# A retention layer's states kept as two 64x64 blocks per pair of heads, with half-array and quarter-array matmuls

## The chip, the cores and the metric

The kernel runs on one core of a Trainium2 chip. The time is device microseconds of that core for one launch; several runs are taken and their median is given. The profile is one execution of the program, recorded by the hardware profiler. Its engines are called PE (TensorE, the matrix engine; PEld are its weight loads), DVE (VectorE), ACT (ScalarE), POOL (GpSimd) and SP (SyncE, which issues transfers).

## The reference

The first half is a linear recurrence over time with a decay per head. Its result, all heads side by side, goes through a two-layer network without bias.

```python
batch, n_heads, seq, head_dim = (4, 8, 768, 64)      # q, k, v, fp32
gamma = 1.0 - 2.0 ** (-5.0 - np.arange(H))
for t in range(S):
    state = gamma * state + einsum('bhd,bhe->bhde', k[:, :, t], v[:, :, t])
    y[:, :, t] = scale * einsum('bhd,bhde->bhe', q[:, :, t], state)
x = y.transpose(0, 2, 1, 3).reshape(B * S, H * D)    # 3072 x 512
h = x @ w_in                                         # 512 x 2048
g = h * tanh(softplus(h))
out = g @ w_out                                      # 2048 x 512, fp32
```

A state belongs to one batch and one head and has 64 x 64 numbers.

## The kernel before

The recurrence is computed in chunks of 128 time steps: 6 chunks per batch, 24 in all, numbered g. The 8 heads are handled as 4 pairs (HP = 4), two heads of 64 side by side on the 128 partitions. Products use 16-bit floats and are summed in fp32 in PSUM. For each chunk:

- `casts` (L211) brings q, k, v to fp16 with the decay multiplied in; POOL does most of it. `turn_k`, `turn` or `turn_by_dma` (L202, L255, L227) transpose q and k.
- `scores` (L266) multiplies k and q of each head: 8 matmuls that use 64 rows of the array, two at a time on different rows. `mask` (L277, DVE) keeps the causal part.
- `outer` (L288) forms k times v over the chunk. Before, one matmul per pair of heads makes a 128x128 block on the whole array. Its diagonal 64x64 blocks are the products of the two heads; the other two blocks mix heads and aren't wanted.
- `state` (L299, DVE) adds the state before (`su`, L306) and multiplies by `gcm` (L307, or L303 alone for the first chunk of a batch and in the first block). `gcm` holds the decay of 128 steps in the diagonal blocks and zero elsewhere, so that it also clears the unwanted blocks. In the first block the state before is added on PE instead, by a matmul with the identity (L296).
- `past` (L310) multiplies the state before with q: one whole-array matmul per pair of heads, 128 columns moving.
- `present` (L317) multiplies the masked scores with v: one matmul per head with a stationary operand of 64 columns, on the left or right half of the array, two side by side.
- ACT copies the sum of past and present from PSUM to `xt` (L349, L358, L400), the input of the network.

The network runs in blocks: the first has 4 chunks, each of the other 10 has 2. `g1` (L405) is the first layer with Mish on ACT (L420). The second layer is `g2_mm` (L424) in blocks 0 to 2. Blocks from 3 on (`SEVEN`) use `seven` (L486), which multiplies 2x2 blocks with seven products and sums `gsum` on DVE (L475 to L484). The sums of the weights are made once (L459 to L462).

The order on each engine is that of the program text; nothing reorders it. The work on chunks stands between the dense matmuls of the block before. Blocks 1 and 2 follow `plan_of` (L646): `scores_two` and `outer_two` among the dense products, then `y_two` (past and present). From block 3 on, `outer_two` comes after the first step of g1, `scores_two` after the fourth, and `y_two` inside `seven`. In the first block (`first_block`, L570) the four chunks go one by one while the weights are still on their way; identity matmuls without use (`spin`, and `spin_quarters`, L247, which works on quarters of the array) keep PE busy there. `last_of_batch` skips the outer product of a batch's last chunk, so that some groups have one chunk and some two. PSUM tiles come from two pools, `mmps` with 4 banks and `atps` with 2 tiles of two banks each, the latter for scores, outer products and y of later chunks.

Of the kernel before, what the change touches and what calls it, by code (L numbers as in the profile page):

```python
# [9 lines left out]
FP16 = mybir.dt.float16  # L10
FP32 = mybir.dt.float32
# [5 lines left out]
def kernel(  # L17
# [9 lines left out]
    nc = tc.nc  # L27
    B, H, S, D = q.shape
    d_model, d_ff = moe_w_in.shape
    P = 128  # L30
    C = 128
    NCH = S // C
    NCK = B * NCH
    HP = H // 2
# [12 lines left out]
    gamma = (1.0 - 2.0 ** (-5.0 - np.arange(H))).astype(np.float64)  # L47
# [7 lines left out]
    cpool = ctx.enter_context(tc.tile_pool(name="rn_const", bufs=1))  # L55
# [4 lines left out]
    stp = ctx.enter_context(tc.tile_pool(name="rn_state", bufs=3))  # L60
# [4 lines left out]
    mmps = ctx.enter_context(  # L65
        tc.tile_pool(name="rn_mmps", bufs=4, space=bass.MemoryType.PSUM))
    atps = ctx.enter_context(
        tc.tile_pool(name="rn_atps", bufs=2, space=bass.MemoryType.PSUM))
# [6 lines left out]
    qs_spread = qvs[:, 2 * H:].rearrange("p (r h) -> p h r", r=CPB)  # L75
    ident = cpool.tile([P, P], FP16, name="ident")
    tri = cpool.tile([P, C], FP32, name="tri")
    gcm = cpool.tile([P, HP, P], FP32, name="gcm")
    warm = cpool.tile([P, 1], FP32, name="warm")
    nc.gpsimd.memset(ident, 0.0)  # L80
    nc.gpsimd.affine_select(  # L81
# [11 lines left out]
        pattern=[[-1, CPB], [-CPB, C // CPB]], channel_multiplier=1)  # L93
    nc.vector.memset(warm, 0.0)
    nc.scalar.activation(warm, warm, AF.Mish)
    nc.vector.memset(gcm, 0.0)
    for h in range(H):
        o = 64 * (h % 2)
        nc.vector.memset(gcm[o:o + 64, h // 2, o:o + 64], float(gamma[h] ** C))

    win_ap = moe_w_in.rearrange("(bp p) f -> p bp f", p=P)
    wout_ap = moe_w_out.rearrange("(fb p) c -> p fb c", p=P)
# [2 lines left out]
    loaded, cast, qkts, ats, ams, states, us, ys = {}, {}, {}, {}, {}, {}, {}, {}  # L105
# [182 lines left out]
    def outer(g, u_ps, onto=None):  # L288
        _, k16, v16, _ = cast[g]
        for i in range(HP):  # L290
            nc.tensor.matmul(  # L291
                u_ps[:, i], k16[:, 2 * i:2 * i + 2], v16[:, 2 * i:2 * i + 2],
                start=onto is None or i == 0, stop=onto is None,
                skip_group_check=onto is not None)
        if onto is not None:
            nc.tensor.matmul(u_ps, ident, onto, start=False, stop=True, skip_group_check=True)  # L296
        us[g] = u_ps

    def state(g):  # L299
        u_ps = us.pop(g)  # L300
        st = stp.tile([P, HP, P], FP16, name="st")
        if g % NCH == 0 or g < CPB:
            nc.vector.tensor_tensor(st, u_ps, gcm, op=ALU.mult)  # L303
        else:
            su = stp.tile([P, HP, P], FP32, name="su")
            nc.vector.tensor_tensor(su, u_ps, states[g - 1], op=ALU.add)  # L306
            nc.vector.tensor_tensor(st, su, gcm, op=ALU.mult)  # L307
        states[g] = st

    def past(g, y, fresh, pairs=range(HP)):  # L310
        st, qt = states[g - 1], qkts[g][0]
        for i in pairs:
            nc.tensor.matmul(  # L313
                y(i), st[:, i], qt[:, i], start=fresh(i), stop=False,
                skip_group_check=True)

    def present(g, y, fresh, pairs=range(HP)):  # L317
        am = ams[g]
# [8 lines left out]
    def last_of_batch(g):  # L327
        return g % NCH == NCH - 1
# [2 lines left out]

    def outer_one(g):
        if not last_of_batch(g):
            outer(g, mmps.tile([P, HP, P], FP32, name="u_ps", tag="mm"), states.get(g - 1))

    def xt_first(g, pairs=slice(None)):
        n = C // CPB
# [3 lines left out]
    def y_one(g):  # L341
        y_ps = mmps.tile([P, HP, C], FP32, name="y_ps", tag="mm")
        inter = g % NCH > 0
        if inter:
            past(g, lambda i: y_ps[:, i], lambda i: i == 0)
        present(g, lambda i: y_ps[:, i], lambda i: not inter and i == 0)
        if g == 0:
            xts[0] = xtp.tile([P, HP, TB], FP16, name="xt")
        nc.scalar.copy(xt_first(g), y_ps.rearrange("p i (r c) -> p i r c", r=CPB))  # L349

    def y_one_in_halves(g):
        n = HP // 2
        y_ps = [mmps.tile([P, n, C], FP32, name="y_ps", tag="mm") for _ in range(2)]
        for k in range(2):
            past(g, lambda i: y_ps[k][:, i % n], lambda i: i % n == 0, range(k * n, (k + 1) * n))
        for k in range(2):
            present(g, lambda i: y_ps[k][:, i % n], lambda i: False, range(k * n, (k + 1) * n))
            nc.scalar.copy(  # L358
                xt_first(g, slice(k * n, (k + 1) * n)),
                y_ps[k].rearrange("p i (r c) -> p i r c", r=CPB))  # L360
# [3 lines left out]
        mask(g)  # L364

    def outer_state(g):
        outer(g, atps.tile([P, 2, HP, P], FP32, name="u_ps", tag="at")[:, 0])
        state(g)


# [8 lines left out]
    def outer_two(blk):  # L379
        a = first[blk]  # L380
        u_ps = atps.tile([P, 2, HP, P], FP32, name="u_ps", tag="at")
        for j in range(2):
            if not last_of_batch(a + j):
                outer(a + j, u_ps[:, j])
        for j in range(2):
            if not last_of_batch(a + j):
                state(a + j)

    def y_two(blk):
        a = first[blk]  # L390
        y_ps = atps.tile([P, HP, 2, C], FP32, name="y_ps", tag="at")
        inter = a % NCH > 0
        if inter:
            past(a, lambda i: y_ps[:, i, 0], lambda i: i % 2 == 0)
        past(a + 1, lambda i: y_ps[:, i, 1], lambda i: not inter and i % 2 == 0)
        for j in range(2):
            present(a + j, lambda i: y_ps[:, i, j], lambda i: False)
        xt = xtp.tile([P, HP, TB], FP16, name="xt")
        xts[blk] = xt
        nc.scalar.copy(  # L400
            xt[:, :, :2 * C], y_ps.rearrange("p i j c -> p i (j c)"))
# [168 lines left out]
    def first_block():  # L570
# [18 lines left out]
        for g in range(CPB):  # L589
            last = g == CPB - 1  # L590
            if not last:
                cast_to(g + 2)
            scores(g)
            mask(g, 2 if last else 1)
            if g > 0:
                y_one(g - 1)
            if not last:
                at_tile(g + 1)
                outer_one(g)
                spin(g + 1, 2 if g else 8)  # L600
                turn_k(g + 1)
                state(g)
                spin_quarters(g + 1, (48, 40, 16)[g], C // 2 if g < 2 else C)
        y_one_in_halves(CPB - 1)
        outer_one(CPB - 1)
        cast_win(0)
        state(CPB - 1)
        for s in range(1, NSL):
# [6 lines left out]
            24: [(turn, CPB)],  # L615
            25: [(scores_one, CPB)],
            27: [(outer_state, CPB)],
            28: [(turn, CPB + 1), (next_chunk, CPB + 2), (next_chunk, CPB + 3)],
            29: [(scores_one, CPB + 1)],
# [26 lines left out]
    def plan_of(blk):  # L646
        a = first[blk] + 4
        if blk >= SEVEN:
            plan = {1: [(cast_to, a + 1), (next_chunk, a)],
                    7: [(cast_to, a + 2), (next_chunk, a + 1)]}  # L650
            if blk + 1 < len(BLOCKS):
                plan[0] = [(outer_two, blk + 1)]
                plan[3] = [(scores_two, blk + 1)]
            return plan
        early, then_seven = blk == 1, blk + 1 == SEVEN
        plan = {1: [(cast_to, a + 1)],
                (1 if early else 2 if then_seven else 4): [(cast_to, a + 1), (next_chunk, a)],
                (5 if early else 8): [(cast_to, a + 2), (next_chunk, a + 1)]}
        plan[10 if early else 7] = [(scores_two, blk + 1)]
        plan[12 if early else 10] = [(outer_two, blk + 1)]  # L660
        plan[14 if early else 13] = [(y_two, blk + 1)]
        return plan
# [58 lines left out]
```

## Time and profile before

| what | value |
|---|---|
| median of 3 runs | 208.84 us (208.76, 208.84, 210.17) |
| span of the profiled execution | 206.5 us; no separate time of that execution is given, and the median is 2.3 us above its span |
| granted PE clock, mean | 0.999 |
| PE busy | 200.1 us in 2005 matmuls |
| first layer, L412 | 88.0 us in 704 matmuls |
| outer products, L291 | 80 matmuls, 219 ns each from issue to end |
| past, L313 | 80 matmuls, 219 ns each |
| present, L323 | 192 matmuls, 219 ns each |
| scores, L273 | 192 matmuls, 216 ns each |
| state, L303, L306, L307 | 7, 13 and 13 operations, 684, 691 and 754 ns each |

Matmuls overlap in the pipeline: a whole-array matmul of 128 columns lasts 219 ns, but the next can start 56 ns later. So what a matmul costs is read from the distance of the starts, and not from its length. Rows such as "128*64 128x128" give the part of the array (rows*columns of the stationary operand) and then the moving operand (partitions x columns).

### The profile page before, as it was taken

The page shows a single profiled execution, that of the slowest core. Times are in us where ns is not written, and L with a number is a line of the kernel's source. Part 1 is how long each engine was busy: PE and PEld are TensorE (multiplying, and loading weights), DVE is VectorE, ACT ScalarE, POOL GpSimd, SP SyncE. Part 2 cuts the span into 40 slices and gives each one's busy share as a digit, 9 for nine tenths or more (in the row PEclk, how much of TensorE's full clock was granted, in tenths as well). Part 3 has the DMA queues.
Part 4 walks back from the last instruction along what each step waited for, and adds up shares of the span by engine and source line. Part 5 has one row for each costly group of instructions (what it writes and reads, how often), then busy time and mean ns, then how long its engine had stood idle before and what let it go on. Part 6 is the DMA issues. An engine that isn't in the chain of part 4 may idle for free.

```text
span 206.5 us, 4747 instructions
## 1 busy us (share of the span) xinstructions
PE 200.1 (97%) x2005; PEld 151.0 (73%) x2005; DVE 120.7 (58%) x184; ACT 86.5 (42%) x146; POOL 76.2 (37%) x72
## 2 busy tenths in 40 slices
PE   7899999999999999999999999999999999999993
PEld 2465444455855865788888888888888888898882
DVE  2697454267019998475585774495675773572062
ACT  2243664142631541453453453453453453552640
POOL 3242000427866555578665265156266000000000
PEclk9999999999999999999999999999999999999999
DMA  5999999999899999999999798499894800200202
GB/s 175 237 219 345 381 387 355 233 296 208 176 205 292 195 228 207 213 238 253 209 218 152 168 195 149 115 246 154 200 241 71 206 0 2 105 0 27 77 25 76
DMA packets 99988, 38.59 MB, mean 187 GB/s; under 512 B 90496, under 2 KB 94080, under 8 KB 99968
## 3 DMA queue, kind: packets, MB, share of 16 engines
q1 hardware_dynamic: 96704, 37.50, 82.4%
q10 hardware_dynamic: 3264, 0.81, 2.4%
q8 instruction: 15, 0.25, 0.5%
q14 instruction: 5, 0.04, 0.1%
HBM read 27.29 MB, written 6.29 MB: 163 GB/s over the span
## 4 chain that ended last, share of the span: by engine, by line
PE 83%; SPq 7%; DMA 5%; DVE 1%; ACT 1%; issue 1%; ACTq 0%
PE h_ps L412 38%; PE o_ps L506 23%; PE o_ps L426 13%; SPq L122 5%; DMA wi<-in_moe_w_in_dram 5%; PE y_ps L323 3%; PE at L273 3%; PE y_ps L313 2%; SPq L140 2%; PE u_ps L291 2%; ACT xt L400 1%; DVE gsum L476 1%; SPq L181 0%; DVE win L157 0%; PE t_ps L261 0%
## 5 line engine op out<-in xcount | busy, mean ns | idle before, releaser
L412 PE MATMUL h_ps<-xt,win 128*128 128x256 f16 (+1 forms) x704 | 88.0, 282 | 0.4 <-ACT xt L400 0.2
L420 ACT ACTIVATE g<-h_ps 128x512 f16<-128x512 f32 x96 | 57.3, 597 | 57.6 <-PE h_ps L412 57.6
L412 PEld LDWEIGHTS <-win 128*128 128x128 f16 x704 | 67.9, 98 | 16.9 <-DVE win L157 0.9
L217 POOL TENSOR_TENSOR qk<-qf,qvs 128x512 f16<-128x512 f32 x20 | 21.5, 1077 | 61.6 <-DMA qf<-in_q_dram 52.3
L283 DVE TENSOR_TENSOR am<-at,tri 128x1024 f16<-128x1024 f32 x20 | 23.7, 1220 | 17.1 <-PE at L273 16.9
L223 POOL TENSOR_TENSOR v<-vf,qvs 128x512 f16<-128x512 f32 x24 | 25.4, 1059 | 18.6 <-DMA vf<-in_v_dram 17.0
L426 PE MATMUL o_ps<-wout,g 128*128 128x512 f16 x128 | 30.1, 380 | 0.0
L222 POOL TENSOR_SCALAR qk<-kf 128x512 f16<-128x512 f32 x18 | 27.7, 1540 | 2.0 <-DMA kf<-in_k_dram 0.7
L506 PEld LDWEIGHTS <-gsum 128*128 128x128 f16 x256 | 24.4, 98 | 3.8 <-DVE gsum L476 0.4
L506 PE MATMUL o_ps<-tmat,gsum 128*128 128x256 f16 x192 | 23.7, 273 | 0.1
L426 PEld LDWEIGHTS <-g 128*128 128x128 f16 x128 | 11.7, 98 | 13.0 <-issue 0.3
L520 DVE TENSOR_TENSOR osb<-o_ps,snap 128x256 f32<-128x256 f32 x24 | 10.1, 422 | 18.8 <-ACT snap L512 15.7
L506 PEld LDWEIGHTS <-g 128*128 128x128 f16 x192 | 18.8, 98 | 2.2
L400 ACT CAST xt<-y_ps 128x1024 f16<-128x1024 f32 x10 | 10.1, 1012 | 21.7 <-PE y_ps L323 21.7
L475 DVE TENSOR_TENSOR gsum<-g 128x512 f16<-128x512 f16 x16 | 7.6, 472 | 13.6 <-ACT g L420 13.6
L506 PE MATMUL o_ps<-wout,g 128*128 128x256 f16 x128 | 15.3, 273 | 0.0
L512 ACT COPY snap<-o_ps 128x256 f32<-128x256 f32 x24 | 8.9, 372 | 14.0 <-PE o_ps L506 14.0
L306 DVE TENSOR_TENSOR su<-u_ps,st 128x512 f32<-128x512 f32 x13 | 9.0, 691 | 4.7 <-PE u_ps L291 4.5
L307 DVE TENSOR_TENSOR st<-su,gcm 128x512 f16<-128x512 f32 x13 | 9.8, 754 | 0.4
L243 PE MATMUL at<-ident 128*128 128x512 f16 (+1 forms) x26 | 8.0, 440 | 1.3 <-POOL ident L81 1.3
L220 ACT ACTIVATE qk<-kf 128x512 f16<-128x512 f32 x6 | 3.8, 630 | 12.4 <-DMA kf<-in_k_dram 12.4
L157 DVE CAST win<-wi 128x1024 f16<-128x1024 f32 x8 | 5.4, 692 | 5.3 <-DMA wi<-in_moe_w_in_dram 5.3
(61 smaller groups left out, 150.0 us busy)
## 6 DMA issues: line engine op xcount, KB each, us to landing
kf<-in_k_dram SPq DMA_DIRECT2D x23, 256.0 KB, 4.9
vf<-in_v_dram SPq DMA_DIRECT2D x23, 256.0 KB, 5.0
out_dram<-osb SPq DMA_DIRECT2D x22, 256.0 KB, 4.0
qf<-in_q_dram SPq DMA_DIRECT2D x19, 256.0 KB, 4.4
wt<-in_moe_w_out_dram SPq DMA_DIRECT2D x3, 1024.0 KB, 10.1
wi<-in_moe_w_in_dram SPq DMA_DIRECT2D x4, 512.0 KB, 6.9
wi<-in_moe_w_in_dram SPq DMA_DIRECT2D x2, 1024.0 KB, 10.3
qfirst<-in_q_dram SPq DMA_DIRECT2D x2, 512.0 KB, 5.0
```

Source lines behind the costliest of these rows:

```text
L122: queue.dma_start(loaded[g][n], (q, k, v)[n][b, :, c * C:(c + 1) * C].rearrange("h p d -> p h d"))
L217: nc.gpsimd.tensor_tensor(q16, qf, qs.unsqueeze(2).broadcast_to((P, H, D)), op=ALU.mult)
L222: nc.gpsimd.tensor_scalar(k16, kf, BOOST, None, op0=ALU.mult)
L223: nc.gpsimd.tensor_tensor(v16, vf, vs.unsqueeze(2).broadcast_to((P, H, D)), op=ALU.mult)
L283: nc.vector.tensor_tensor(am[:, :, i:i + n], at[:, :, i:i + n], keep.unsqueeze(1).unsqueeze(1).broadcast_to((P, 2, n, C)), op=ALU.mult)
L307: nc.vector.tensor_tensor(st, su, gcm, op=ALU.mult)
L400: nc.scalar.copy(xt[:, :, :2 * C], y_ps.rearrange("p i j c -> p i (j c)"))
L412: nc.tensor.matmul(h_ps[:, j], wins[s][f // 2][:, bp, f % 2 * P:(f % 2 + 1) * P], xts[blk][:, bp, :nt], start=(bp == 0), stop=(bp == NBP - 1))
L420: nc.scalar.activation(gt, h_ps, AF.Mish, scale=inv_boost3)
L426: nc.tensor.matmul(o_ps, gts[blk, fb][:, t * P:(t + 1) * P], wouts[s][:, f, cols], start=(fb == 0), stop=(fb == NFB - 1))
L506: nc.tensor.matmul(o_ps, x(f), w(f), start=first and f == 0, stop=f == n - 1, skip_group_check=True)
L520: nc.vector.tensor_tensor(dst, o_ps, plus, op=ALU.add)
```

## The change

A state is kept as 64 columns on 128 partitions: the upper 64 partitions hold one head of the pair, the lower 64 the other. The two unwanted blocks are no longer computed or stored.

- `outer`: two matmuls per pair of heads instead of one, each with 64 stationary columns (one half of the array) and 64 moving columns instead of 128. PE issues 160 of these instead of 80.
- `past`: two matmuls per pair of heads instead of one, each on 64 rows and 64 columns of the array (a quarter), the moving operand still 128 columns. 160 instead of 80.
- `state`, and the identity matmul of the first block: 256 columns instead of 512.
- `gcm` has 256 columns and needs no memset to zero ahead.

The order on the other engines and all transfers stay as they were.

```diff
-    gcm = cpool.tile([P, HP, P], FP32, name="gcm")
+    gcm = cpool.tile([P, HP, D], FP32, name="gcm")
...
-    nc.vector.memset(gcm, 0.0)
     for h in range(H):
         o = 64 * (h % 2)
-        nc.vector.memset(gcm[o:o + 64, h // 2, o:o + 64], float(gamma[h] ** C))
+        nc.vector.memset(gcm[o:o + 64, h // 2], float(gamma[h] ** C))
...
     def outer(g, u_ps, onto=None):
         _, k16, v16, _ = cast[g]
         for i in range(HP):
-            nc.tensor.matmul(
-                u_ps[:, i], k16[:, 2 * i:2 * i + 2], v16[:, 2 * i:2 * i + 2],
-                start=onto is None or i == 0, stop=onto is None,
-                skip_group_check=onto is not None)
+            for hh in range(2):
+                nc.tensor.matmul(
+                    u_ps[64 * hh:64 * hh + 64, i], k16[:, 2 * i + hh], v16[:, 2 * i + hh],
+                    start=i == 0, stop=onto is None, skip_group_check=True)
...
-        st = stp.tile([P, HP, P], FP16, name="st")
+        st = stp.tile([P, HP, D], FP16, name="st")
...
-            su = stp.tile([P, HP, P], FP32, name="su")
+            su = stp.tile([P, HP, D], FP32, name="su")
...
     def past(g, y, fresh, pairs=range(HP)):
         st, qt = states[g - 1], qkts[g][0]
         for i in pairs:
-            nc.tensor.matmul(
-                y(i), st[:, i], qt[:, i], start=fresh(i), stop=False,
-                skip_group_check=True)
+            for hh in range(2):
+                o = slice(64 * hh, 64 * hh + 64)
+                nc.tensor.matmul(
+                    y(i)[o], st[o, i], qt[o, i], start=fresh(i), stop=False,
+                    skip_group_check=True)
...
-            outer(g, mmps.tile([P, HP, P], FP32, name="u_ps", tag="mm"), states.get(g - 1))
+            outer(g, mmps.tile([P, HP, D], FP32, name="u_ps", tag="mm"), states.get(g - 1))
...
-        outer(g, atps.tile([P, 2, HP, P], FP32, name="u_ps", tag="at")[:, 0])
+        outer(g, atps.tile([P, 2, HP, P], FP32, name="u_ps", tag="at")[:, 0, :, :D])
...
-                outer(a + j, u_ps[:, j])
+                outer(a + j, u_ps[:, j, :, :D])
```

## The prediction, made before the result was known

> **What bounds the kernel now.** I read the page first: busy shares, the slices, the chain that ended last.
>
> ```profile
> span 206.5 us, 4747 instructions
> PE 200.1 (97%) x2005; PEld 151.0 (73%) x2005; DVE 120.7 (58%) x184; ACT 86.5 (42%) x146; POOL 76.2 (37%) x72
> PEclk9999999999999999999999999999999999999999
> PE 83%; SPq 7%; DMA 5%; DVE 1%; ACT 1%; issue 1%; ACTq 0%
> ```
>
> The matrix engine (PE) carries 83% of the chain at full granted clock; VectorE, which does the state sums, carries 1%. So the change is worth what it does to PE's own stream, and where. The chain in order of time gives the place:
>
> ```profile
> 16.44 9.41 DMA wi<-in_moe_w_in_dram
> 25.88 0.70 DVE win L157
> 26.63 7.08 PE h_ps L412 x32
> ```
>
> Up to 26.6 us the chain runs through the weight loads; PE waits for the cast of win there. From 26.63 on it is PE almost without a break. What PE does between the dense products is seen in its timeline (start, length, line, operation, array rows*columns, moving shape, count):
>
> ```profile
> 60.85 0.62 PE L273 MATMUL at<-qkt 64*128 64x128 f16 x16
> 61.40 1.90 PE L426 MATMUL o_ps<-wout,g 128*128 128x512 f16 x8
> 63.14 0.61 PE L291 MATMUL u_ps<-v,qk 128*128 128x128 f16 x8
> 63.59 1.89 PE L426 MATMUL o_ps<-wout,g 128*128 128x512 f16 x8
> 65.31 0.39 PE L313 MATMUL y_ps<-qkt,st 128*128 128x128 f16 x4
> 65.63 0.64 PE L323 MATMUL y_ps<-am,v 128*64 128x128 f16 x16
> 66.20 1.04 PE L426 MATMUL o_ps<-wout,g 128*128 128x512 f16 x4
> ```
>
> Lengths overlap, so I use start to start. Eight outer products, full array, neighbours full array: 63.14 to 63.59, 0.45 us, 0.056 each. Four past products: 65.31 to 65.63, 0.32 where 4 x 0.056 = 0.22; the missing 0.10 comes where the array goes from 128*128 to 128*64. Sixteen present products on half arrays: 65.63 to 66.20, 0.57, where eight pairs side by side at 0.056 make 0.45; the missing 0.12 is a slow first pair and the way back to 128*128. So one excursion from full array to half array and back costs about 0.22 us beyond its stream. Eight past and sixteen present products elsewhere say the same:
>
> ```profile
> 94.04 0.61 PE L313 MATMUL y_ps<-qkt,st 128*128 128x128 f16 x8
> 94.58 0.64 PE L323 MATMUL y_ps<-am,v 128*64 128x128 f16 x16
> 95.15 1.05 PE L506 MATMUL o_ps<-tmat,gsum 128*128 128x256 f16 x8
> ```
>
> 94.04 to 95.15 is 1.11 us; the stream is 16 x 0.056 = 0.90; the rest is 0.21. (The first product after it is 0.01 late too, in the starts of the trace, which makes 0.22.) A quarter-array stream of 64 columns stands in the first block:
>
> ```profile
> 11.38 0.58 PE L251 MATMUL at<-ident 64*64 64x64 f16 x48
> 11.97 0.40 PE L273 MATMUL at<-qfirst_t,kt 64*128 64x128 f16 x8
> ```
>
> 48 quarters, four side by side: the last ends at 11.96 and one takes 0.193, so starts spread over 0.39: 12 fours at 0.032 us.
>
> **The change part by part.** *Outer products.* After 26.63 there are ten groups in the chain: four of 4 matmuls (44.5, 84.6, 130.4, 176.0 us) and six of 8 (63.3, 77.8, 99.7, 115.1, 145.5, 160.6), 64 in all, each between full-array products. The stream becomes 64 pairs of 64 columns. No row has this pair. Its bounds: 0.028, half the 0.056 of the 128-column pair, and 0.056, if something other than the columns sets it (the 64-column weight loads of L323 last 109 ns, the 128-column ones of L291 98). I take 0.032, from the quarter matmuls of L251, which load 64 columns of weights and stream 64 columns, as here. Each group gains an excursion, 0.22. A group of 4: 4 x 0.032 + 0.22 = 0.35 against 0.22, +0.13. A group of 8: 8 x 0.032 + 0.22 = 0.48 against 0.45, +0.03. Sum 4 x 0.13 + 6 x 0.03 = +0.70 us. With pairs at 0.028 it is 64 x 0.004 = 0.26 less; at 0.056 64 x 0.024 = 1.54 more.
>
> *Past products.* Ten groups after 26.63 (blocks 1 to 10), 68 full matmuls, become 136 quarter matmuls in pairs, upper left and lower right quarter, still 128 moving columns. Pairs of L273 and L323 with 128 columns keep 0.056, so the stream is unchanged. The order full, half, full becomes full, quarter, half, full: one change of array shape more per group. Every change between shapes in these rows costs about 0.10 with a slow first pair of 0.02: 10 x 0.117 = +1.17 us. From 64*64 to 128*64 the trace has no row; nearest is 64*128 to 128*64 at 12.15 to 12.29 us (11.97 and 4 x 0.056 give 12.20, then 0.09 of nothing). Bounds: 0, if a change between two column-split shapes is free, and 0.117; I take the upper, which is nearest. The Trainium skill, TensorEngine Tiling, Key Properties, says that a change of tiling mode, not merely of the tile, empties the array; by it the term stays 1.17, without it 0.
>
> *First block (before 26.6).* Its three y groups go scores (64*128), past, present: the number of changes stays. Outer products of chunks 1 to 3 follow present products, now in the same shape: a change less going in, one more coming out. The group of chunk 0 gains a change, while PE waits about 0.36 us for v. The identity matmul of L296 loses half of 512 columns three times. I set all this to 0: PE's wait before 26.63 (0.22 us in the starts of the trace) and the DMA behind it hide either sign. Without that cover it would be about +0.1.
>
> *VectorE.* 33 state operations go from 512 to 256 columns. The nearest rows are copies out of PSUM: L432 with 512 columns 686 ns, L518 with 256 columns 425. 33 x 0.26 = 8.6 us of VectorE go, and the 0.49 us memset of gcm. In the waits of before no PE instruction waits for L303, L306 or L307; worth 0 on the chain. One VectorE wait lies on it: gsum L476 before 109.23 us, 1.15 us long instead of some 0.45 while GpSimd ran beside it, about 0.32 us of idle PE.
>
> ```profile
> 107.68 1.22 POOL L223 TENSOR_TENSOR v<-vf,qvs 128x512 f16<-128x512 f32 x1
> 108.03 1.15 DVE L476 TENSOR_TENSOR gsum<-gsum,g 128x512 f16<-128x512 f16 x1
> 109.23 0.33 PEld L506 LDWEIGHTS <-gsum 128*128 128x128 f16 x4 [0.42 <-DVE gsum L476]
> ```
>
> It may vanish or come in another block, as the engines shift: 0, between -0.32 and +0.32.
>
> *Waits and queues.* The instruction lists of the two kernels are the same on ScalarE, GpSimd and SyncE, and no wait is added; nothing is moved past another DMA. What queues behind the emptied array is the next dense product, and behind that ScalarE's Mish, which is idle 58% of the time.
>
> **Sum.** 0.70 + 1.17 = +1.87 us. The profiled span of 206.5 becomes 208.4. The median, 208.84, is 2.3 us more than that span, which I take as the work around it; no separate time of the profiled execution is given, and the runs lie from 208.76 to 210.17. 208.84 + 1.87 = 210.7 us, 0.9% slower.
>
> **Rivals.** (a) *Half pairs set by their weight loads*, 0.056 a pair: +1.54, 212.3 us. For it: loads of 64 columns last longer than those of 128. Against it: L251 gets four such loads through in 0.032.
>
> (b) *Quarters that don't run side by side.* In the past products both row halves now write the same bank, in different partitions. In L273 the two row halves write different banks, in L251 too, so no row excludes that the pair is serialised: 68 x 0.056 = +3.8 more, 214.5 us. For it: only the absence of a row. Against it: L323's column halves share a bank at 0.056 a pair. The Trainium skill, TensorEngine Tiling, Restrictions and Gotchas, says that different row tiles can't access one PSUM bank at the same time; taken literally it gives this rival's time. No run here shows it so far.
>
> (c) *Quarter to half is free*: 208.84 + 0.70 = 209.5 us. Against it: each change of shape in the rows costs the same, also that between row-split and column-split.
>
> (d) *Faster.* The change of shape is hidden for the outer products too, because one half's weights are loaded while the other still streams. Then only streams count: 64 x 0.024 = -1.54, and the shorter VectorE queue takes away the stall at 109.23, -0.32: 207.0 us, 0.9% faster. It decides from where an excursion costs less than 0.15 us per group. Against it: L313 to L323 pays at all ten places after 26.6.
>
> **How the numbers follow.** Forecast (210.3 to 211.1, by the stall's 0.3 and some 0.1 of reading): 0.60; (a) 0.16; (b) 0.08; (c) 0.11; (d) 0.05. The range leaves out (b) and (d): from (c) less 0.1, 209.4, to (a) plus 0.1, 212.4. One per cent, about what a measurement can tell here, is 2.09 us: slower by that means above 210.93. A third of the forecast's chance lies there, 0.20; with (a) and (b) 0.44. Faster than 206.75 needs (d) and more: 0.03. The rest, 0.53, is within 1%.
>
> **What would show it.** In the timeline of after: outer groups of 16 half matmuls with a gap of 0.1 us ahead and 0.37 from their first start to the next dense product; 0.56 there shows (a), no gap (d). Past groups: 0.45 for 8 pairs, then a gap of 0.1 ahead of the present products; 0.9 shows (b), no gap shows (c). State operations of about 0.4 us with nobody waiting for them. PE reaching line 412 after the win cast at about 26.6 as before. The prediction is wrong if these gaps are hidden, or if a wait for VectorE or GpSimd appears in front of the dense products.

## The result, and the profile after

| | before | after |
|---|---|---|
| median | 208.87 us (4 runs, 208.76 to 210.17) | 210.91 us (4 runs, 210.57 to 212.13) |
| ratio | | 1.0109, 95% interval 1.0067 to 1.0151 |
| span of the profiled execution | 206.5 us | 208.8 us |

The changed kernel is slower by 2.04 us. The forecast was 1.87 us, a time of 210.7 and a range of 209.4 to 212.4. The interval of the ratio holds 1.01, so that "slower by over 1%" and "within 1%" stay undecided. The two spans differ by 2.3 us, more than the medians: where a run has both its time and its span, the time is about 1.8 us longer (210.57 and 208.8 here, 208.91 and 207.1 for the kernel before in a second profiled run), so the first profiled execution of the kernel before was a short one. The 2.3 us that the prediction took as the work around the span are therefore too many; its sum goes from median to median and doesn't use them.

The page of the changed kernel: span, busy shares, clock and the chain by engine. (Its line numbers differ by one from those before: past is L314, present L324, g1 L413, g2 L427, the seven products L507, scores L272; the outer products stay L291.)

```profile
span 208.8 us, 5066 instructions
PE 202.4 (97%) x2165; PEld 148.9 (71%) x2165; DVE 109.5 (52%) x183; ACT 86.6 (41%) x146; POOL 76.5 (37%) x72
...
PEclk9999999999999999999999999999999999999999
...
PE 80%; DMA 8%; SPq 7%; ACT 2%; DVE 1%; issue 1%; ACTq 0%
```

The clock is the same. The chain now takes a load of k beside PE's work from 34.2 to 40.8 us, hence 3% less PE and more DMA; PE waits for that chunk (`qk`, ahead of the transposes at 41 us) about 0.2 us in both traces. VectorE has lost 11.2 us of work (120.7 to 109.5), and the span grew all the same. The place is PE's timeline. A stretch of the changed kernel with the work on the chunks of block 2 (start, length, line, array, moving operand, count):

```profile
61.54 0.62 PE L272 MATMUL at<-qkt 64*128 64x128 f16 x16
62.09 1.90 PE L427 MATMUL o_ps<-wout,g 128*128 128x512 f16 x8
63.92 0.44 PE L291 MATMUL u_ps<-v,qk 128*64 128x64 f16 x16
64.29 1.90 PE L427 MATMUL o_ps<-wout,g 128*128 128x512 f16 x8
66.12 0.41 PE L314 MATMUL y_ps<-qkt,st 64*64 64x128 f16 x8
66.47 0.64 PE L324 MATMUL y_ps<-am,v 128*64 128x128 f16 x16
```

From the dense group at 62.09 to the outer products at 63.92 it is 1.83 us; before it was 61.40 to 63.14, 1.74. These 0.09 are the gap ahead of the new shape. The outer products then take 0.37 to the next dense start, instead of 0.45: eight pairs at 0.032 make 0.26, and the slow first pair and the way back add 0.11. From there to the past products it is 1.83 again, instead of 1.72: 0.1 ahead of the quarters and 0.01 for the late first product. Past to present is 0.35 instead of 0.32, although the shape was already a split one: going from quarters to halves costs like any other change.

For the chunks of block 4 the past products are eight pairs:

```profile
95.24 0.63 PE L314 MATMUL y_ps<-qkt,st 64*64 64x128 f16 x16
95.80 0.64 PE L324 MATMUL y_ps<-am,v 128*64 128x128 f16 x16
96.37 1.92 PE L507 MATMUL o_ps<-tmat,gsum 128*128 128x256 f16 x16
```

95.24 to 95.80 is 0.56, where eight pairs at 0.056 make 0.45; serialised quarters would need 0.90. PE's wait for gsum is there once more, in another block:

```profile
139.72 1.04 POOL L222 TENSOR_TENSOR v<-vf,qvs 128x512 f16<-128x512 f32 x1
139.89 1.15 DVE L477 TENSOR_TENSOR gsum<-gsum,g 128x512 f16<-128x512 f16 x1
141.10 0.33 PEld L507 LDWEIGHTS <-gsum 128*128 128x128 f16 x4 [0.43 <-DVE gsum L477]
```

It moved from the sums of block 4 to those of block 6 and kept its size, 0.33 us of PE against 0.32. So it adds nothing to the difference.

### The profile page after: what moved, and what is told of

Same layout as the page of the kernel before. It is cut to its first block, busy times and chain, and to the rows that moved or that the text cites. A ratio compares the mean times of both kernels' runs of the same rounds, so it can differ in the third digit from the quotient of the medians.

```text
span 208.8 us, 5066 instructions
## 1 busy us (share of the span) xinstructions
PE 202.4 (97%) x2165; PEld 148.9 (71%) x2165; DVE 109.5 (52%) x183; ACT 86.6 (41%) x146; POOL 76.5 (37%) x72
## 4 chain that ended last, share of the span: by engine, by line
PE 80%; DMA 8%; SPq 7%; ACT 2%; DVE 1%; issue 1%; ACTq 0%
PE h_ps L413 38%; PE o_ps L507 23%; PE o_ps L427 10%; SPq L121 5%; DMA wi<-in_moe_w_in_dram 5%; DMA kf<-in_k_dram 3%; PE y_ps L324 3%; PE at L272 3%; PE y_ps L314 2%; SPq L139 2%; PE u_ps L291 2%; ACT xt L401 1%; DVE gsum L477 1%; SPq L180 0%; DVE win L156 0%
## 5 line engine op out<-in xcount | busy, mean ns | idle before, releaser
L413 PE MATMUL h_ps<-xt,win 128*128 128x256 f16 (+1 forms) x704 | 88.2, 282 | 0.9 <-DVE win L156 0.5
L413 PEld LDWEIGHTS <-win 128*128 128x128 f16 x704 | 67.5, 98 | 17.7 <-DVE win L156 1.5
L427 PE MATMUL o_ps<-wout,g 128*128 128x512 f16 x128 | 30.2, 380 | 0.0
L507 PEld LDWEIGHTS <-gsum 128*128 128x128 f16 x256 | 24.4, 98 | 3.8 <-DVE gsum L477 0.4
L507 PE MATMUL o_ps<-tmat,gsum 128*128 128x256 f16 x192 | 23.7, 273 | 0.2 <-DVE gsum L477 0.2
L427 PEld LDWEIGHTS <-g 128*128 128x128 f16 x128 | 11.6, 98 | 13.1 <-issue 0.3
L507 PEld LDWEIGHTS <-g 128*128 128x128 f16 x192 | 18.8, 98 | 2.2
L507 PE MATMUL o_ps<-wout,g 128*128 128x256 f16 x128 | 15.3, 273 | 0.0
L242 PE MATMUL at<-ident 128*128 128x512 f16 (+1 forms) x26 | 8.6, 466 | 1.3 <-POOL ident L81 1.3
L433 DVE COPY osb<-o_ps 128x512 f32<-128x512 f32 x8 | 5.3, 686 | 6.2 <-PE o_ps L427 6.2
L477 DVE TENSOR_TENSOR gsum<-gsum,g 128x512 f16<-128x512 f16 x16 | 8.1, 508 | 0.5
```

The source lines that it names most:

```text
L413: nc.tensor.matmul(h_ps[:, j], wins[s][f // 2][:, bp, f % 2 * P:(f % 2 + 1) * P], xts[blk][:, bp, :nt], start=(bp == 0), stop=(bp == NBP - 1))
L427: nc.tensor.matmul(o_ps, gts[blk, fb][:, t * P:(t + 1) * P], wouts[s][:, f, cols], start=(fb == 0), stop=(fb == NFB - 1))
L477: nc.vector.tensor_tensor(s2, s1, a11, op=ALU.subtract)
L507: nc.tensor.matmul(o_ps, x(f), w(f), start=first and f == 0, stop=f == n - 1, skip_group_check=True)
```

## The experiments

For each kernel its trace gives two numbers beside the median. One is the start of the second layer in block 0, up to which the weights' transfers pace the kernel. The other, called the dense stretch here, runs from the first dense product behind the first transposes of chunk 4 (41.31 us in the kernel before) to the start of the last block's seven products (197.02), less PE's waits for gsum and for the transposes' copy qkt. Before: 197.02 - 41.31 - 0.33 = 155.39.

| kernel | median, us | ratio, 95% interval | second layer starts | waits for gsum | dense stretch | against before |
|---|---|---|---|---|---|---|
| before | 208.87 | | 33.55 | 0.32 | 155.39 | |
| before again | 208.91 (1 run) | | 34.17 | 0.33 | 155.39 | 0.00 |
| after | 210.91 | 1.0109 (1.0067 to 1.0151) | 33.98 | 0.33 | 157.26 | +1.87 |
| after again | 210.43 (1 run) | | 33.59 | 0.32 | 157.26 | +1.87 |
| past products only | 210.29 | 1.0062 (1.0043 to 1.0081) | 33.39 | 0.93 | 156.56 | +1.17 |
| outer products only | 210.46 | 1.0067 (1.0038 to 1.0096) | 33.85 | 1.17 | 156.08 | +0.69 |
| the same again | 209.91 (1 run) | | 33.61 | 0.92 | 156.08 | +0.69 |
| three more changes of shape | 213.09 | 1.0182 (1.0146 to 1.0217) | 34.21 | 0.43 | 159.53 | +4.14 |
| after, outer joined to present | 209.08 | 1.0013 (0.9986 to 1.0039) | 34.01 | 0.06 | 155.67 | +0.28 |
| before, half outer joined | 208.12 | 0.9974 (0.9960 to 0.9988) | 33.55 | 0.32 | 154.50 | -0.89 |
| states in two | 208.85 | 1.0010 (0.9992 to 1.0028) | 33.56 | 0.05 | 155.65 | +0.26 |
| joined from block 3 | 208.78 | 0.9983 (0.9959 to 1.0007) | 33.53 | 0.89 | 154.64 | -0.75 |
| states twice | 215.36 | 1.0298 (1.0262 to 1.0334) | 35.10 | 0.43 | 159.18 | +3.79 |

The ratios are to runs of the kernel before beside each: 208.94 us for the four from the past products to the first joined kernel, 208.75 for the next two, 209.18 for the last two.

**The past products alone**, on the kernel before:

```diff
-            nc.tensor.matmul(
-                y(i), st[:, i], qt[:, i], start=fresh(i), stop=False,
-                skip_group_check=True)
+            for hh in range(2):
+                o = slice(64 * hh, 64 * hh + 64)
+                nc.tensor.matmul(
+                    y(i)[o], st[o, i, o], qt[o, i], start=fresh(i), stop=False,
+                    skip_group_check=True)
```

> Only the past products are split into quarter matmuls; outer products, states and state sums stay as before (the quarters read the diagonal blocks of the 128-column states). Theory (each change of the array's shape empties it and costs about 0.117 us, the matmuls themselves cost nothing more): ten groups after the first block with one change more each, +1.17 us, about 210.0 us, and no stretch of PE longer but these ten. Rival (the added matmuls and weight loads cost by their number, 2.04 us over 320 added instructions): 160 added instructions, +1.0 us, spread over the pairs of the past products as starts further apart than 56 ns. If the first block's 0.43 us belongs to the change, the second layer of the first block starts later than at 33.55 us.

The dense stretch grew by 1.17 us: ten changes at 0.117. The median grew by 1.35, with 0.6 us more of waits for gsum. The quarters still run at 0.056 a pair, so the added time is not spread over the instructions, as the rival has it, which would have made about as much, 1.0. For the chunks of block 4 the past products begin at 94.58 and the present ones at 95.14, 0.56 as in the changed kernel:

```profile
94.58 0.63 PE L315 MATMUL y_ps<-qkt,st 64*64 64x128 f16 x16
95.14 0.64 PE L325 MATMUL y_ps<-am,v 128*64 128x128 f16 x16
```

**The outer products alone**; states keep 128 columns, their other blocks are zeroed once:

```diff
+            for hh in range(2):
+                o = slice(64 * hh, 64 * hh + 64)
+                nc.tensor.matmul(
+                    u_ps[o, i, o], k16[:, 2 * i + hh], v16[:, 2 * i + hh],
+                    start=i == 0, stop=onto is None, skip_group_check=True)
...
+            for o in halves:
+                nc.vector.tensor_tensor(st[o, :, o], su[o, :, o], gcm[o, :, o], op=ALU.mult)
```

> Only the outer products are split into half-array matmuls of 64 columns; past products and 128-column states stay as before. The halves write the diagonal blocks, and each state operation is issued as two, one for each block of 64 partitions, with the other blocks of the states cleared once; so VectorE does about 0.15 us more for each, not less. Theory: ten excursions of 0.22 us against 64 pairs that each stream 0.024 us less, +0.69 us, about 209.6 us. Rival (cost by number of added instructions): 160 added, +1.0 us. If VectorE's shorter state sums were a part of the balance, this kernel would lose them and stand further above before than theory says.

The dense stretch grew by 0.69, as the theory has it, and 1.17 + 0.69 is the 1.87 of the whole change. But the median stands 1.5 us above before, further than the theory has it, as in the last sentence of the expectation: PE waited 1.17 us for gsum and 0.39 for qkt. It also came to the first layer later, at 20.02 us instead of 19.49 (19.68 in the second execution below), behind a wait of 0.29 us for a mask of VectorE. The wait for qkt is VectorE's doing. The state operations on 64 partitions now take from 44.88 to 46.69 what took 44.76 to 46.09:

```profile
44.88 0.88 DVE L314 TENSOR_TENSOR su<-u_ps,st 64x256 f32<-64x256 f32 x2 [0.85 <-PE u_ps L297]
45.78 0.87 DVE L317 TENSOR_TENSOR st<-su,gcm 64x256 f16<-64x256 f32 x2
46.69 0.69 DVE L267 COPY qkt<-t_ps 128x1024 f16<-128x1024 f16 x1
```

A second execution of the same kernel, for the waits for gsum:

> The kernel with the outer products alone in halves, profiled a second time. Its gsum waits came to 1.17 us and its wait for qkt to 0.39. If they belong to its longer state sums, they come again within 0.3 us; if they belong to where GpSimd's casts fall in one execution, the gsum waits come out anywhere between 0 and 1.2 us.

0.92 us for gsum and 0.39 for qkt. That lies within the 0.3 of the one theory and within the range of the other, so it doesn't decide between them.

**Three more changes of shape in the kernel before**, by idle quarters with zero weights ahead of each chunk's present products:

```diff
         for j in range(2):
+            quarters(a + 1, y_ps)
             present(a + j, lambda i: y_ps[:, i, j], lambda i: False)
```

> The kernel before, with one idle pair of quarter matmuls (64 columns, weights of zero, so that the sums stay) ahead of the present products of each of the two chunks in the ten later y groups. That is three changes of the array's shape more in each group and 40 instructions more in all. Theory: 30 changes at about 0.117 us, +3.5 us, with the idle pairs' stream some 0.1 to 0.6 more: 212.4 to 213.0 us. Rival (cost by number of instructions): 40 x 0.006 = +0.3 us, and 20 pairs at 0.03 make 0.6: at most 209.8 us.

```profile
95.89 0.61 PE L316 MATMUL y_ps<-qkt,st 128*128 128x128 f16 x8
96.43 0.22 PE L396 MATMUL y_ps<-qkt,zeros 64*64 64x64 f16 x2
96.58 0.41 PE L326 MATMUL y_ps<-am,v 128*64 128x128 f16 x8
96.92 0.22 PE L396 MATMUL y_ps<-qkt,zeros 64*64 64x64 f16 x2
97.07 0.41 PE L326 MATMUL y_ps<-am,v 128*64 128x128 f16 x8
97.42 0.28 PE L518 MATMUL o_ps<-tmat,gsum 128*128 128x256 f16 x1
```

95.89 to 97.42 is 1.53 us, against 1.11 in the kernel before. Two matmuls of 64 columns that do no work hold up PE by 0.15 us each time. 4.14 us over 30 changes is 0.138, the 0.117 and the idle pairs' stream. The median grew by 4.15 us, to just above the expected 213.0. The rival of the number of instructions has fallen: it had at most 0.9 us for the 40 more of them.

**The changed kernel with outer products behind present products** (called joined from here on). Of `outer_two` only the state sums stay in the first step of the next block:

```diff
-                plan[0] = [(outer_two, blk + 1)]
+                plan[0] = [(states_two, blk + 1)]
...
-            seven(blk, [] if last else [(y_two, blk + 1)], last)
+            seven(blk, [(f, blk + n) for f, n in ((y_two, 1), (outer_two, 2))
+                        if blk + n < len(BLOCKS)], last)
```

> The changed kernel with the outer products of blocks 3 to 10 issued right behind the present products of the block before, so that both use the half-array shape in one excursion; their state sums stay where they were on VectorE. Same instructions in another order on PE. Theory: eight of the ten excursions of 0.22 us go, -1.76 us from 210.91, about 209.15 us. Rival (cost by number of added instructions): no difference from the changed kernel, 210.9 us. A third way: the outer products now wait for the casts of k and v on GpSimd, and the gain is lost in a wait of PE inside the seven products.

The kernel joins seven groups, those of blocks 4 to 10, and not the eight that the expectation counts. The dense stretch went down by 1.59 us, 0.227 for each of the seven; with eight excursions at 0.22 the expectation had 1.76. The same matmuls, in an order with fewer changes, bring the changed kernel back to the time of before. That the median, 209.08, is so near to the expected 209.15 is in part luck: one group fewer was joined, and PE waited 0.27 us less for gsum. No wait for the casts showed.

```profile
95.17 0.63 PE L315 MATMUL y_ps<-qkt,st 64*64 64x128 f16 x16
95.74 0.64 PE L325 MATMUL y_ps<-am,v 128*64 128x128 f16 x16
96.21 0.42 PE L292 MATMUL u_ps<-v,qk 128*64 128x64 f16 x16
96.56 1.70 PE L513 MATMUL o_ps<-tmat,gsum 128*128 128x256 f16 x14
```

Present to outer has no gap: 0.47 for eight pairs of 128 columns, 0.35 for eight of 64 and the way back.

**The kernel before with joined half-array outer products** (the outer products alone, in the order of the last kernel):

> Half-array outer products in the kernel before (whole-array past products, 128-column states, each state operation issued as two), with the outer products of blocks 3 to 10 right behind the present products of the block before. Theory: those 52 pairs stream 0.024 us less each and pay for no change of shape, -1.25 us; the two outer groups that stay alone cost +0.16. So PE's stream is 1.1 us shorter than before. VectorE's longer state sums made PE wait about 0.85 us for gsum and 0.39 for qkt in the kernel with the outer products alone; if that comes again, 208.9 + 0.1; if not, 207.8 us. Rival (cost by number of added instructions): at least 210 us.

208.12 us, a quarter of a per cent faster than before (0.9974, interval 0.9960 to 0.9988). With seven groups instead of eight the theory gives: a joined group of two chunks 0.196 less, one of one chunk 0.099 less, 4 x 0.196 + 3 x 0.099 = 1.08 (present and outer products of a large group took 0.570 + 0.447 in the starts of the trace and take 0.471 + 0.350), and 0.19 for the three groups that stay alone: -0.89, as measured. The 0.39 for qkt is still there.

**State operations in two**, to put the waits for gsum on VectorE's load:

> The kernel before with each state operation issued as two of half the columns; nothing else differs, and all matmuls are the same. Theory (VectorE has a price at the margin, the sums gsum and the copy qkt are the places): PE's waits for gsum and qkt grow from 0.32 us to about 1 to 1.5, +0.7 to +1.2 us, about 209.9 us. Rival (those waits come from where GpSimd's casts fall, not from VectorE's load): PE waits within 0.4 us of before, 208.9 us, and the excess of the kernel with half outer products alone stays unexplained.

The time is that of before, and the waits for gsum fell to 0.05. But the run hardly loaded VectorE (122.0 us busy instead of 120.7): the second of two independent halves begins before the first has ended, and the pair takes as long as the one operation did.

```profile
44.78 0.76 DVE L309 TENSOR_TENSOR su<-u_ps,st 128x256 f32<-128x256 f32 x2 [0.83 <-PE u_ps L291]
45.45 0.75 DVE L312 TENSOR_TENSOR st<-su,gcm 128x256 f16<-128x256 f32 x2
46.12 0.68 DVE L263 COPY qkt<-t_ps 128x1024 f16<-128x1024 f16 x1
```

So it says only that gsum waits differ from kernel to kernel with hardly a difference in load. Its 0.26 in the dense stretch is one wait for the transposed q and k, a transfer. The state operations are doubled in the last kernel below.

**Half-array outer products in eight joined groups only**, the rest as before:

> The kernel before, with half-array outer products only where they stand right behind present products: eight groups, of blocks 3 to 10 (block 3 joined too). The first two later groups keep whole-array outer products and one state operation for both heads. Theory: a joined group of two chunks takes 0.196 us less than before, one of one chunk 0.099, as the seven joined groups have shown; 5 x 0.196 + 3 x 0.099 = -1.28 us of PE stream, and the wait of 0.39 for the copy qkt is not there. About 207.5 us, against 208.75 for before. Rival (VectorE's split state sums or GpSimd's casts take the gain back in waits): 208.1 us or more.

The rival won: 208.78 us, and with an interval of 0.9959 to 1.0007 no difference from before. The stream is shorter still, but PE waits 0.89 us for gsum, 0.22 for transposed q and k, and 0.4 at the outer products of block 3, which now come before the cast of their v has ended (PE, then GpSimd):

```profile
66.18 0.29 PE L307 MATMUL u_ps<-v,qk 128*64 128x64 f16 x8
66.74 0.32 PE L307 MATMUL u_ps<-v,qk 128*64 128x64 f16 x8 [0.27 <-POOL v L228]
```
```profile
65.64 1.04 POOL L228 TENSOR_TENSOR v<-vf,qvs 128x512 f16<-128x512 f32 x1 [0.40 <-DMA vf<-in_v_dram]
```

**State operations issued twice:**

> The kernel before with the 26 state operations that follow the first block's (su and st of the chunks that are not the first of a batch) issued twice, the second time with the same result: some 18 us more of VectorE and no other difference. Theory that VectorE's load is off the chain up to a margin: the copy qkt of chunk 5 comes 1.4 us later and PE waits for it about 1.3 us; elsewhere the masks and sums have the room, so at most +1.3 and the scatter of the gsum waits (0.05 to 1.2 us), 210 us. Rival (VectorE's load makes the gsum waits): 0.3 us or more in each of the five blocks in which the casts run, +3 us in all, about 211.5 us.

+6.2 us (215.36 against 209.18), more than either expected, and not by gsum, which took 0.43. From the waits of that kernel:

```profile
PE at L273 <- DVE su L307: 3.1, 2, 1.6
PEld L273 <- DVE qkt L263: 2.3, 2, 1.9
PEld L508 <- DVE gsum L478: 0.6, 2, 0.4
```

The scores need the PSUM tile of the outer products, and that comes free only when VectorE has read it. For the chunks of block 6 the second su ends at 122.89 instead of about 120.7 us (three operations of 0.72 from 118.56 on), 2.2 us later, and PE waits 1.7 of these:

```profile
121.47 1.42 DVE L307 TENSOR_TENSOR su<-u_ps,st 128x512 f32<-128x512 f32 x2
```
```profile
121.08 0.40 PE L273 MATMUL at<-qkt 64*128 64x128 f16 x8
123.03 0.40 PE L273 MATMUL at<-qkt 64*128 64x128 f16 x8 [1.55 <-DVE su L307]
```

The same wait comes once more, at 170.62, and a past product waits 0.3 us for its state. The copy qkt, which has no such room, makes PE wait 1.45. With 0.1 us more for gsum these are 5.3 of the 6.2 us. In the profiled execution the second layer also starts 1.5 us later, with the landing of the weights; nothing of the edit runs before it, and why the weights came later there stays open. So the state sums have about 0.5 us of room ahead of the scores and none ahead of qkt: halving them is worth nothing, doubling them a lot.

**Both kernels again:**

> The kernel before, unchanged, profiled a second time. It tells what of the 2.3 us between the two spans is scatter between executions. If the start of the second layer (33.55 us before, 33.98 after) moves by some 0.4 us and PE's wait for gsum by some 0.3 us between executions of the same kernel, both are scatter; the groups of outer, past and present products should repeat to 0.01 us.

> The changed kernel, unchanged, profiled a second time. If the later start of the second layer belongs to the change, it lies at 33.9 to 34.0 us again; if it is the landing of the weights, it can lie anywhere from 33.4 to 34.2, as in the kernels seen so far. From that start to the first matmul of the last second-layer group it should be 165.04 us and the gsum waits again.

The dense stretches repeat to 0.01 us. The start of the second layer does not: 33.55 and 34.17 before, 33.98 and 33.59 after. It follows the landing of the weights: in all four executions it comes 7.67 us after the start of the fifth cast of win (25.88 and 26.50 before, 26.31 and 25.92 after), which waits for that landing. Between the two kernels it shows no difference beyond this scatter. The 165.04 us from there on came out 0.25 longer in the changed kernel's second execution. All of that lies ahead of the dense stretch, in a longer wait of the chunk 4 transposes for ScalarE's cast of k.

## Why the prediction was right

*Outer products, +0.70.* Measured +0.69. The unknown price, a pair of half-array matmuls with 64 columns, was taken as 0.032 from the quarter matmuls, between bounds of 0.028 and 0.056; in the starts of the trace it is 0.031 to 0.032. Rival (a), 0.056 by the weight loads, fell: these loads last 111 ns each on average and don't set the pace.

*Past products, +1.17.* Measured +1.17. The step from 64*64 to 128*64, which no row had shown and for which the prediction took its upper bound, costs like the others, so (c) fell. The Trainium skill, TensorEngine Tiling, Key Properties, had said that a change of tiling mode empties the array; the traces agree, with about 0.117 us for each. Rival (b) fell too: pairs of quarters keep 0.056 us. The sentence of the Trainium skill, TensorEngine Tiling, Restrictions and Gotchas, that different row tiles cannot access one PSUM bank at the same time does not hold here as it stands: these quarters share the bank but no partition, and run side by side.

*Faster, (d).* Fell at its condition: an excursion costs 0.22 us and was to cost less than 0.15.

*First block, 0.* Nothing of the change reaches the end of it; the wait for the weights takes it up. At 27.06 and 26.67 us PE still waits 0.69 and 0.27 us for the cast of win in the two traces of the changed kernel (0.22 and 0.82 before). The cover is thin: in the kernel with the outer products alone, which came 0.53 us later to the first layer, nothing of this wait was left.

*VectorE, 0.* The relief (11.2 us, forecast 9.1) was worth nothing, as said: the dense stretch grew by the two terms of PE and by nothing else. That the wait for gsum stayed at 0.33 us, in both traces of the changed kernel, is luck. The prediction allowed it to change by 0.32 us either way, and it was 0.05 to 1.17 in the other kernels, one of which differs only in its past products (0.93). What the prediction left out is how little room there is on the other side, 0.5 us or none.

*The rest.* 2.04 - 1.87 = 0.17 us are less than the scatter of one kernel's profiled executions (0.62 us in the start of the second layer, before and before again). What sets the waits for gsum is only partly settled. In the thirteen traces every sum of line 476 that takes 0.7 us or more instead of 0.43 (40 of 208) lies beside a GpSimd cast, and after the last cast none is slow. A cast beside it is not enough, though: 44 more of these sums run for 0.3 us or more beside one and take 0.43. Whether the two engines hold each other up, and why the kernel with split outer products had about 1 us of such waits twice, was not tested by itself.

## What to carry to other kernels

Count the changes of the array's shape, not the multiplications saved: in a group of eight outer products the shorter stream saved 0.19 us here, and the excursion from full to split and back cost 0.22. Half-array matmuls pay where they can stand next to others of the same shape; then their shorter stream can be a gain (0.9974 of before with seven groups; with eight the waits took it back). Before moving work to make that so, look at which cast or copy its operands come from, since a wait of 0.4 us eats several such gains.

## What the hardware showed beyond what was expected

Two independent VectorE operations of 256 columns on 128 partitions, one behind the other, took 0.67 us from start to next start (44.78 to 45.45), about as long as one of 512 columns (0.72, 44.76 to 45.48). The sum and the product together took 1.34 us in halves and 1.33 whole. On 64 partitions each pair of halves took 0.90. A single one of 256 columns lasts 0.42. So splitting an operation was free here where both halves used all partitions.
